# Splitting half of the first part's input weights into fp32r pairs, with the low parts made by GpSimd

## The chip, the cores and the metric

One core of a Trainium2 chip runs the whole program. The metric is the device time of one execution in microseconds; the kernel before was timed three times, with a median of 418.88 us (417.71 to 420.25).

## The reference

```python
# attention: for each of B=4 batches, H=8 heads, S=768 steps, D=48
y[:, :, t] = r_t @ (state + (u * k_t) v_t^T)
state      = w_t[:, None] * state + k_t v_t^T
# then, on x = y as (B*S=3072 rows, 384):
h   = max(x @ w1, x @ w2, x @ w3)        # 384 -> 768
out = h @ w_out                          # 768 -> 384
```

All inputs are float32, except that the four matrices may arrive as float64; the profile is of that form (384 KB a load of 128x384 values).

## The kernel before, in words

The rows of x are worked on in six parts of 512 rows. A part (`half` in the code) needs four chunks of 128 steps of attention. Attention of a chunk k is a list of lettered steps: b, s, f two scans on VectorE, r products of keys and receptances with the scans, d, D, e the diagonal term (e ends with two `affine_select` on GpSimd into `a`), X scores on TensorE, M `copy_predicated` of the scores into `a` on VectorE, T transposes of the keys on TensorE with a ScalarE copy into `kn`, R and V, Z the three products into `y`, U the state's product into `pu`, S its decay on VectorE, E the ScalarE copy of y into x with six small DMAs, n the load of a later chunk's `tin`. V and Z are two passes over the same banks; the first product of Z waits for a `nop` that waits for the last product of V.

The matrix product of a part is cut into 18 groups (a tile f of 128 of the 768 columns, times w1, w2, w3) and the output products behind them. A group's PSUM tile `psm` comes from a pool of three banks. ScalarE copies the first of three groups (L130), VectorE takes the maximum with the other two (L133); this is put out one group later (`behind`). The first part multiplies in plain fp32 (`wval`, `x`, `plain`), three products a group. The other five split x and the weights into a high and a low fp32r part, nine products a group: hi·hi, hi·lo, lo·hi. `split` makes the high part by a ScalarE cast (L110) and the low by a VectorE subtraction (L111).

Each of 24 weight tiles (18 of input, 6 of output) is loaded as raw float64 by SP (`load_w`, letter w), prepared on ScalarE (`split_w1`, L303, letter i), decoded by two VectorE instructions (`split_w2`, L312 and L314; letter c does both for the next one), and later split (`split_w3`, letter f or `fix`). Before, `fix` is called five times behind the groups of the first part, and for the rest in the second part; the loop in `group` spreads the 24 over its 18 groups.

The order on every engine is written out by hand: FRONT for the first chunks, with warm-up products W, then START (letters m for a group, c for a decode, a for a unit of attention), then a loop that puts out groups and units in step. TURN and ORD are a turn of attention cut into units by "|". The `w_p` pool holds raw, decoded and split tiles in a ring.

Of the kernel before, what the change touches and what calls it, by code (L numbers as in the profile page):

```python
# [29 lines left out]
F32 = mybir.dt.float32  # L30
# [4 lines left out]
ALU = mybir.AluOpType  # L35
# [16 lines left out]
HT = 512  # L52
HC = C // 2
CPH = HT // C
SOON = HT - C
# [8 lines left out]
NST = 3  # L64
WARM = 10
XD, LEAD = -2, 0

FRONT = ("b0 s0 f0 d0 W2 D0 W3 r0 X0 T0 W3 c0 e0 b1 s1 d1 D1 U0 f1 W4 R0 e1 M0 V0 Z0 E0 S0 n3 w r1 "  # L70
# [3 lines left out]
TURN = "b1 d1 w | f1 w | D1 r1 c1 | e1 M0 w | "  # L74
ORD = "w R0 V0 U0 X1 Z0 E0 b2 d2 | f2 n3 w | D2 S0 r2 c2 | e2 M1 w | T1 w | |"

# [18 lines left out]
def kernel(ctx: ExitStack, tc, tin, nat, u_flat, u_pair, v_t, w_all, out, ytr):  # L95
# [5 lines left out]

    w_p = ctx.enter_context(tc.tile_pool(name="w", bufs=NW + 1))
    whi, wlo, wval, verdict = [], [], [], []
    acc = const.tile([128, LINE], F32, name="acc")[:, 0:NK]
    wacc = const.tile([128, LINE], F32, name="wacc")[:, 0:NW]
    flag = const.tile([1, LINE], I32, name="flag")[:, 0:1]

    def split(hi, lo, src, later=None):

        nc.scalar.copy(out=hi, in_=src)  # L110
        rest = lambda: nc.vector.tensor_tensor(out=lo, in0=src, in1=hi.bitcast(F32), op=ALU.subtract)  # L111
        rest() if later is None else later.append(rest)
# [4 lines left out]

    def moe_groups(x_hi, x_lo, pools, store, first=0):

# [30 lines left out]
        for f in range(FT):  # L150
            for wi in range(3):
# [10 lines left out]
                ps = ps_m.tile([128, HT], F32, name="psm")  # L162
                n = 0
                for ct in range(KT):
                    terms = ((wval, x_hi),) if plain else ((whi, x_hi), (whi, x_lo), (wlo, x_hi))
                    for wt, xt in terms:
                        nc.tensor.matmul(ps[:, :], lhsT=wt[f * 3 + wi][:, ct * 128:(ct + 1) * 128], rhs=xt[:, ct, :],  # L167
                                         start=(n == 0), stop=(n == KT * len(terms) - 1))
                        n += 1
# [26 lines left out]
    with ExitStack() as fast:  # L196
# [138 lines left out]
        def split_w3(i):  # L335

            w = w_p.tile([128, 2, PC], F32R, name="w")
            whi.append(w[:, 0, :])
            wlo.append(w[:, 1, :])
            split(whi[i], wlo[i], wval[i], wrest)  # L340

# [124 lines left out]
        def transposes(k):  # L466
            if goes_on(k):
                p = prep[k]
                pt = ps_tu.tile([128, 512], F32, name="tu")
                for pr in range(NP):  # L470
# [47 lines left out]
        def values(k, second=False):  # L518
# [16 lines left out]
            if not second and k >= CPH:  # L535
                p["first"] = after(nc.gpsimd.nop(nofuse=True), mm)  # L536

# [51 lines left out]
        def x_parts(half):  # L589
            x = xt[half]  # L590
            if half < PLAIN:
                return x, None
            x_hi = xs_p.tile([128, KT, HT], F32R, name="x_hi")
            x_lo = xs_p.tile([128, KT, HT], F32R, name="x_lo")
            later = []
            for ct in range(KT):
                split(x_hi[:, ct, :], x_lo[:, ct, :], x[:, ct, :], later)
            flush(later)
            return x_hi, x_lo

# [27 lines left out]
        def fix():  # L628
# [3 lines left out]
            if fixed < NW:  # L632
                split_w3(fixed)
            if flush_one:
# [40 lines left out]
        def group():  # L675
            nonlocal groups, mg
            half = groups // GPH
            if groups % GPH == 0 and (half or not mg):
# [9 lines left out]

                mg = moe_groups(*xs[half], pools, store, 0 if half else SOON)
                if half == 0:  # L690
                    return
            g = groups % GPH
            while done < (NW if half or g >= 3 * FT else g + 1):
                weights()
            while half >= PLAIN and fixed <= NW and (half > PLAIN or fixed < 1 + min(NW, -(-(g + 1) * NW // (3 * FT)))):
                fix()
# [192 lines left out]
```

## Time and profile before

| | |
|---|---|
| median of 3 runs | 418.88 us |
| profiled execution, its time | 418.33 us |
| its span, first to last instruction | 416.5 us |
| mean granted TensorE clock | 0.991 |
| TensorE busy | 404.1 us, 97% |
| VectorE busy | 276.7 us, 66% |
| ScalarE busy | 151.1 us, 36% |
| GpSimd busy | 76.2 us, 18% |

The shares are means over the span. In the page, PE is TensorE's products, PEld its weight loads, DVE is VectorE, ACT ScalarE, POOL GpSimd, and a q behind a name is its queue. The first part's groups run from 36.8 to 95.7 us, its output products to 115.2 us.

### The profile page before, as it was taken

How to read it: one execution, taken by the hardware profiler on the slowest of the kernel's cores; microseconds unless marked ns; L12 is line 12 of the kernel's file. 1: busy time of each engine (PE TensorE's matmuls, PEld its weight loads, DVE VectorE, ACT ScalarE, POOL GpSimd, SP SyncE). 2: the span in 40 equal slices, each digit the busy share in tenths (PEclk: the TensorE clock that was granted, in tenths of full speed). 3: DMA queues.
4: the chain of work that ended last, by engine and by line, in shares of the span. 5: the costliest groups of instructions: out<-in, count | busy, mean ns of one | idle time of the engine just before them, and what ended most of it. 6: DMA issues, size and time to landing. Idle time of an engine off the chain costs nothing.

```text
span 416.5 us, 9217 instructions
## 1 busy us (share of the span) xinstructions
PE 404.1 (97%) x3761; PEld 317.9 (76%) x3761; DVE 276.7 (66%) x515; ACT 151.1 (36%) x318; POOL 76.2 (18%) x92
## 2 busy tenths in 40 slices
PE   6989999999999999999999999999999999999995
PEld 3657545546678888987888988889988888888894
DVE  6977998878869968836868558677757532223310
ACT  1343524142545434425334535533623321312211
POOL 3410111013331231311321311421222200000000
PEclk9978999999999999999999999999999999999999
DMA  8982973452380412295644596752460000300002
GB/s 211 329 226 90 331 208 134 133 174 58 88 253 3 126 48 79 61 295 178 201 152 146 121 285 204 210 172 76 134 210 2 2 2 0 97 0 2 1 1 79
DMA packets 23839, 53.30 MB, mean 128 GB/s; under 512 B 3281, under 2 KB 9745, under 8 KB 23793
## 3 DMA queue, kind: packets, MB, share of 16 engines
q1 hardware_dynamic: 19872, 42.65, 33.9%
q10 hardware_dynamic: 3920, 10.03, 7.6%
q8 instruction: 30, 0.49, 0.5%
q14 instruction: 17, 0.13, 0.1%
HBM read 46.77 MB, written 4.72 MB: 124 GB/s over the span
## 4 chain that ended last, share of the span: by engine, by line
PE 90%; DMA 3%; ACT 2%; issue 1%; DVE 1%; SPq 1%; ACTq 0%; DVEq 0%; POOLq 0%
PE psm L167 55%; PE psm L187 14%; PE gram L451 5%; PE y L529 5%; PE tu L494 3%; PE y L484 3%; PE tu L471 2%; PE psm L575 1%; PE psm L413 1%; DMA x<-x 1%; SPq L556 1%; PE psm L147 1%; DMA out_dram<-m 1%; DMA tin<-in_tin_dram 1%; ACT x_hi L110 0%
## 5 line engine op out<-in xcount | busy, mean ns | idle before, releaser
L167 PE MATMUL psm<-x_hi,w 128*128 128x512 f32 x540 | 172.6, 394 | 0.5 <-ACT m L130 0.3
L167 PEld LDWEIGHTS psm<-x_hi,w 128*128 128x128 f32 x540 | 101.4, 188 | 22.6 <-ACT m L191 0.8
L167 PE MATMUL psm<-x_lo,w 128*128 128x512 f32 x270 | 105.2, 390 | 0.0
L133 DVE TENSOR_TENSOR m<-psm,m 128x512 f32<-128x512 f32 x60 | 41.2, 686 | 59.6 <-PE psm L167 44.6
L187 PE MATMUL psm<-w,h_hi 128*128 128x384 f32 x288 | 78.1, 364 | 0.0
L429 POOL TENSOR_SCALAR_AFFINE_SELECT a<-cs 64x512 f32<-64x512 f32 x48 | 37.2, 776 | 159.9 <-DVE cs L423 81.0
L167 PEld LDWEIGHTS psm<-x_lo,w 128*128 128x128 f32 x270 | 50.7, 188 | 9.8
L187 PEld LDWEIGHTS psm<-w,h_hi 128*128 128x128 f32 x288 | 51.8, 188 | 6.5 <-DVE w L314 0.4
L547 ACT COPY x<-y 112x512 f32<-112x512 f32 x24 | 14.1, 586 | 82.0 <-PE y L529 81.6
L167 PE MATMUL psm<-x,w 128*128 128x512 f32 x96 | 43.1, 599 | 0.0
L187 PE MATMUL psm<-w,h_lo 128*128 128x384 f32 x120 | 40.3, 335 | 0.0
L393 ACT ACTIVATE gf<-gf 112x1034 f32<-112x1034 f32 x24 | 25.7, 1070 | 34.4 <-DVE tin L388 34.0
L110 ACT CAST h_hi<-m 128x512 fp32r<-128x512 f32 x30 | 18.6, 622 | 53.7 <-DVE m L133 53.7
L404 POOL TENSOR_TENSOR kr<-kr 128x384 f32<-128x384 f32 x16 | 18.8, 1178 | 92.3 <-PE y L529 87.2
L376 DVE TENSOR_TENSOR_SCAN gf<-tin,d_fwd 112x517 f32<-112x517 f32 x24 | 34.9, 1453 | 0.7
L362 DVE TENSOR_TENSOR_SCAN gf<-tin,d_bwd 112x517 f32<-112x517 f32 x24 | 29.9, 1246 | 5.1 <-DMA tin<-in_tin_dram 5.1
L167 PEld LDWEIGHTS psm<-x,w 128*128 128x128 f32 x96 | 17.6, 190 | 19.5 <-issue 18.9
L111 DVE TENSOR_TENSOR h_lo<-m,h_hi 128x512 fp32r<-128x512 f32 x30 | 20.7, 689 | 17.4 <-ACT h_hi L110 17.4
L460 DVE COPY_PREDICATED a<-mask,gram 128x384 f32<-128x384 int32 x48 | 25.3, 582 | 2.5 <-PE gram L451 2.5
L529 PE MATMUL y<-a,v 64*64 64x128 f32 (+3 forms) x768 | 26.2, 251 | 0.5 <-POOLq L536 0.2
L529 PEld LDWEIGHTS y<-a,v 64*64 64x64 f32 (+1 forms) x768 | 22.2, 129 | 4.8 <-issue 2.4
L130 ACT COPY m<-psm 128x512 f32<-128x512 f32 x30 | 17.5, 582 | 16.6 <-PE psm L167 12.2
(72 smaller groups left out, 424.9 us busy)
## 6 DMA issues: line engine op xcount, KB each, us to landing
tin<-in_tin_dram SPq DMA_DIRECT2D x23, 448.0 KB, 5.6
w<-in_w_all_dram SPq DMA_DIRECT2D x24, 384.0 KB, 7.7
cv<-in_w_all_dram ACTq DMA_DIRECT2D x24, 384.0 KB, 3.4
kr<-in_nat_dram SPq DMA_DIRECT2D x16, 384.0 KB, 5.5
tin<-in_tin_dram SPq DMA_DIRECT2D x23, 231.0 KB, 4.2
v<-in_nat_dram SPq DMA_DIRECT2D x24, 192.0 KB, 6.0
out_dram<-m SPq DMA_DIRECT2D x24, 192.0 KB, 2.1
x<-x SPq DMA_DIRECT2D x30, 32.0 KB, 2.0
```

Of the source, the lines that this page charges most:

```text
L111: rest = lambda: nc.vector.tensor_tensor(out=lo, in0=src, in1=hi.bitcast(F32), op=ALU.subtract)
L133: nc.vector.tensor_tensor(out=m[:, :], in0=ps[:, :], in1=m[:, :], op=ALU.max)
L167: nc.tensor.matmul(ps[:, :], lhsT=wt[f * 3 + wi][:, ct * 128:(ct + 1) * 128], rhs=xt[:, ct, :], start=(n == 0), stop=(n == KT * len(terms) ...
L187: nc.tensor.matmul(pss[tt][:, 0:DM], lhsT=ht[f][:, tok], rhs=wt[FT * 3 + f][:, :], start=(f == 0 and i == 0), stop=(f == FT - 1 and i == l ...
L362: nc.vector.tensor_tensor_scan(out=gf[0:112, 0, ::-1], data0=t[0:112, 0:WC][:, ::-1], data1=d_bwd[0:112, ::-1], initial=0.0, op0=ALU.mult, ...
L376: nc.vector.tensor_tensor_scan(out=gf[0:112, 1, :], data0=tbuf[k % NB][0:112, 0:WC], data1=d_fwd[0:112, :], initial=0.0, op0=ALU.mult, op1 ...
L393: nc.scalar.activation(out=flat, in_=flat, func=AF.Square, accum_out=acc[0:112, k:k + 1])
L404: nc.gpsimd.tensor_tensor(out=n[:, 0, :], in0=n[:, 0, :], in1=n[:, 1, :], op=ALU.mult)
L429: nc.gpsimd.affine_select(out=a[rows, :, 0:2, :], pattern=[[0, 4], [0, 2], [1, HC]], in_=cs[rows, :].rearrange("p (a b) -> p a b", b=2).un ...
L451: nc.tensor.matmul(to, lhsT=p["kp"][q:q + 48, pr, lo:lo + HC], rhs=p["rp"][q:q + 48, pr, HC * late:C], start=(hh, lo) not in begun, stop=T ...
L460: nc.vector.copy_predicated(out=p["a"][:, 2 * hh:2 * hh + 2, :, :].rearrange("p a b c -> p a (b c)"), mask=mask_b(2), data=p["gs"][hh].rea ...
L529: mm = nc.tensor.matmul(p["y"][64 * half:64 * half + m, hh, j, HC * late:C], lhsT=natt[k][0][lo:lo + HC, h * D:h * D + m], rhs=a[:, j, :] ...
```

## The change

In the first part, groups from f = 3 on (weights 9 to 17) multiply split operands, as the later parts do: nine fp32r products in place of three fp32 ones. Their maxima, the intermediate h and the output products of the first part stay plain. The high parts of these nine weights and of the first part's x are cast on ScalarE, the low ones subtracted on GpSimd. x is split ahead of group 6, weight 9 + j ahead of group 7 + j, and for that the decode of weight 10 + j must have been put out. The remaining weights are split later in the order 0 to 8, 18 to 23, by VectorE as before.

Besides: two weight loads in FRONT are put out later; U of a turn moves from its first unit to its third, T from the fifth to the third, behind U; T's bank comes from the pool of the groups for k > 4; the `nop` between V and Z is on SP for chunks 4 to 7; `w_p` has one buffer more.

```diff
+LATE = 3
-FRONT = (... "b0 s0 ... E0 S0 n3 w r1 "
-         "W2 X1 ... S1 w n4 w i i i r2 " ...
-         "W3 X3 d4 T3 R3 M3 x V3 Z3 E3 U3 p p w w ..."
+FRONT = (... "b0 s0 ... E0 S0 n3 r1 "
+         "W2 X1 ... S1 n4 w i i i r2 " ...
+         "W3 X3 d4 T3 R3 M3 x w V3 Z3 E3 w U3 p p w w ..."
-ORD = "w R0 V0 U0 X1 Z0 E0 b2 d2 | f2 n3 w | D2 S0 r2 c2 | e2 M1 w | T1 w | |"
+ORD = "w R0 V0 X1 Z0 E0 b2 d2 | f2 n3 w | D2 U0 T1 S0 r2 c2 | e2 M1 w | w | |"
...
+    late = FT if w_all.dtype == F32 else LATE
+    nl = 3 * (FT - late)
-    def split(hi, lo, src, later=None):
+    def split(hi, lo, src, later=None, eng=nc.vector):
         nc.scalar.copy(out=hi, in_=src)
-        rest = lambda: nc.vector.tensor_tensor(out=lo, in0=src, in1=hi.bitcast(F32), op=ALU.subtract)
+        rest = lambda: eng.tensor_tensor(out=lo, in0=src, in1=hi.bitcast(F32), op=ALU.subtract)
...
+                if plain and f == late:
+                    x_hi, x_lo = parts()
-                    terms = ((wval, x_hi),) if plain else ((whi, x_hi), (whi, x_lo), (wlo, x_hi))
+                    terms = ((wval, x_hi),) if x_lo is None else ((whi, x_hi), (whi, x_lo), (wlo, x_hi))
...
-            split(whi[i], wlo[i], wval[i], wrest)
+            split(whi[i], wlo[i], wval[i], *(None, nc.gpsimd) if 3 * late <= i < 3 * FT else (wrest,))
...
-                pt = ps_tu.tile([128, 512], F32, name="tu")
+                pt = ps_m.tile([128, HT], F32, name="psm") if k > CPH else ps_tu.tile([128, 512], F32, name="tu")
...
-                p["first"] = after(nc.gpsimd.nop(nofuse=True), mm)
+                p["first"] = after((nc.sync if k < 2 * CPH else nc.gpsimd).nop(nofuse=True), mm)
...
+        def split_x(half):
+            x = xt[half]
...
-                split(x_hi[:, ct, :], x_lo[:, ct, :], x[:, ct, :], later)
+                split(x_hi[:, ct, :], x_lo[:, ct, :], x[:, ct, :], later, nc.vector if half else nc.gpsimd)
             flush(later)
...
-                split_w3(fixed)
+                split_w3(fixed + 3 * late if fixed < nl else fixed - nl if fixed < 3 * FT else fixed)
...
-            while half >= PLAIN and fixed <= NW and (half > PLAIN or fixed < 1 + min(NW, -(-(g + 1) * NW // (3 * FT)))):
+            due = nl + g + 1 if nl else -(-(g + 1) * NW // (3 * FT))
+            while half >= PLAIN and fixed <= NW and (half > PLAIN or fixed < 1 + min(NW, due)):
+                fix()
+            if nl and not half and g == 3 * late - 3:
+                split_x(0)
+            while not half and fixed < min(nl, g - 3 * late + 3):
+                while done < min(NW, NW - 13 + fixed):
+                    weights()
                 fix()
```

## Rows read from the trace of the kernel before

**Rows 1.** The page, busy time of each engine over the span.
```profile
PE 404.1 (97%) x3761; PEld 317.9 (76%) x3761; DVE 276.7 (66%) x515; ACT 151.1 (36%) x318; POOL 76.2 (18%) x92
```

**Rows 2.** The chain of waits: start us, length us, what; a stall, plain groups, split groups.
```profile
25.38 1.79 issue
...
66.83 10.50 PE psm L167 x24
...
120.49 10.47 PE psm L167 x45
```

**Rows 3.** Stretches: length, PE, PEld, DVE, ACT, POOL busy, granted clock, DMA share, GB/s.
```profile
57.54:104.40 46.86, 46.86 (x385) 25.06 (x387) 39.87 (x78) 15.64 (x32) 8.57 (x10) 1.00 0.38 119
...
27.16:33.66 6.50, 6.38 (x74) 4.30 (x75) 2.60 (x7) 0.58 (x1) 0.00 (x0) 0.50 0.48 145
...
120.00:180.00 60.00, 60.00 (x551) 51.91 (x542) 48.66 (x87) 26.65 (x57) 13.49 (x16) 1.00 0.31 90
```

**Rows 4.** VectorE's instructions in order of time: start us, length us.
```profile
94.83 1.25 DVE L314 SCALAR_TENSOR_TENSOR w<-w,cv 128x384 uint32<-128x384 uint32 x1
...
98.73 0.56 DVE L314 SCALAR_TENSOR_TENSOR w<-w,cv 128x384 uint32<-128x384 uint32 x1
...
100.22 1.23 DVE L376 TENSOR_TENSOR_SCAN gf<-tin,d_fwd 112x517 f32<-112x517 f32 x1
...
103.35 1.05 DVE L460 COPY_PREDICATED a<-mask,gram 128x384 f32<-128x384 int32 x2
...
183.35 0.69 DVE L133 TENSOR_TENSOR m<-psm,m 128x512 f32<-128x512 f32 x1 [4.06 <-ACT m L130]
...
306.18 1.99 DVE L376 TENSOR_TENSOR_SCAN gf<-tin,d_fwd 112x517 f32<-112x517 f32 x1
```

**Rows 5.** GpSimd's instructions in order of time, beside two of these.
```profile
183.10 1.01 POOL L405 TENSOR_TENSOR kr<-kr,u_bc 128x384 f32<-128x384 f32 x1
...
306.07 1.00 POOL L404 TENSOR_TENSOR kr<-kr 128x384 f32<-128x384 f32 x1 [9.66 <-PE y L529]
```

**Rows 6.** TensorE in order of time, the first product of V.
```profile
104.52 0.57 PE L529 MATMUL y<-a,v 64*64 64x128 f32 x16
```

**Rows 7.** Groups by line and shape: busy us, mean ns, idle before them and releaser.
```profile
L133 DVE TENSOR_TENSOR h_hi<-psm,h_hi 128x512 f32<-128x512 f32 x12 | 8.2, 687 | 4.8 <-PE psm L167 4.7
L460 DVE COPY_PREDICATED a<-mask,gram 128x384 f32<-128x384 int32 x48 | 25.3, 582 | 2.5 <-PE gram L451 2.5
L111 DVE TENSOR_TENSOR w<-w 128x384 fp32r<-128x384 f32 x24 | 13.1, 557 | 3.8 <-ACT w L110 3.8
L110 ACT CAST w<-w 128x384 fp32r<-128x384 f32 x24 | 11.6, 513 | 0.0
L110 ACT CAST x_hi<-x 128x512 fp32r<-128x512 f32 x15 | 8.3, 616 | 1.1 <-DMA x<-x 1.1
```

**Rows 8.** Waits: who for whom, us in total, times, longest us.
```profile
DVE cv L312 <- ACT cv L303: 1.9, 3, 1.0
...
PEld psm L167 <- ACT m L191: 0.8, 1, 0.8
...
PE y L529 <- POOLq L536: 0.2, 1, 0.2
```

**Rows 9.** SP's own waits, the loads of `tin` behind R.
```profile
SPq L241 <- PE y L484: 79.9, 9, 15.1
```

**Rows 10.** SP's issues in order of time, the two loads that move.
```profile
12.41 0.35 SPq L287 DMA_DIRECT2D w<-in_w_all_dram  x1
...
16.02 0.42 SPq L287 DMA_DIRECT2D w<-in_w_all_dram  x1
```

**Rows 11.** The instruction queue in 16.0:16.5, 24.5:25.0 and 30.5:31.0: packets, MB, share of 16 engines.
```profile
q8 instruction: 1, 0.02, 16.0%
q8 instruction: 1, 0.02, 14.3%
q8 instruction: 1, 0.02, 13.0%
```

More of the change, by code (lines that the diff above doesn't have):

```diff
@@ L65 @@
 WARM = 10
+LATE = 3
 XD, LEAD = -2, 0
-FRONT = ("b0 s0 f0 d0 W2 D0 W3 r0 X0 T0 W3 c0 e0 b1 s1 d1 D1 U0 f1 W4 R0 e1 M0 V0 Z0 E0 S0 n3 w r1 "
[1 row of a table removed]
+FRONT = ("b0 s0 f0 d0 W2 D0 W3 r0 X0 T0 W3 c0 e0 b1 s1 d1 D1 U0 f1 W4 R0 e1 M0 V0 Z0 E0 S0 n3 r1 "
[1 row of a table added]
          "W4 X2 d3 D3 T2 c2 b3 s3 e3 R2 U2 n5 w M2 V2 Z2 E2 f3 S2 r3 "
[1 row of a table removed]
[1 row of a table added]
 TURN = "b1 d1 w | f1 w | D1 r1 c1 | e1 M0 w | "
-ORD = "w R0 V0 U0 X1 Z0 E0 b2 d2 | f2 n3 w | D2 S0 r2 c2 | e2 M1 w | T1 w | |"
+ORD = "w R0 V0 X1 Z0 E0 b2 d2 | f2 n3 w | D2 U0 T1 S0 r2 c2 | e2 M1 w | w | |"
 START = ("mcamcamcamcamcamcaamca"
@@ L100 @@
     const = ctx.enter_context(tc.tile_pool(name="const", bufs=1))
-    w_p = ctx.enter_context(tc.tile_pool(name="w", bufs=NW + 1))
-    whi, wlo, wval, verdict = [], [], [], []
+    w_p = ctx.enter_context(tc.tile_pool(name="w", bufs=NW + 2))
+    whi, wlo, wval, verdict = [None] * NW, [None] * NW, [], []
+    late = FT if w_all.dtype == F32 else LATE
+    nl = 3 * (FT - late)
     acc = const.tile([128, LINE], F32, name="acc")[:, 0:NK]
@@ L116, in flush, with moe_groups @@
             later.pop(0)()
-    def moe_groups(x_hi, x_lo, pools, store, first=0):
+    def moe_groups(x_hi, x_lo, pools, store, first=0, parts=None):
         plain = x_lo is None
@@ L337, in split_w3 @@
             w = w_p.tile([128, 2, PC], F32R, name="w")
-            whi.append(w[:, 0, :])
-            wlo.append(w[:, 1, :])
-            split(whi[i], wlo[i], wval[i], wrest)
+            whi[i], wlo[i] = w[:, 0, :], w[:, 1, :]
+            split(whi[i], wlo[i], wval[i], *(None, nc.gpsimd) if 3 * late <= i < 3 * FT else (wrest,))
         wrest = []
@@ L592, in x_parts @@
                 return x, None
+            return split_x(half)
+        xsplit = {}
+        def split_x(half):
+            x = xt[half]
             x_hi = xs_p.tile([128, KT, HT], F32R, name="x_hi")
@@ L596, in x_parts @@
             for ct in range(KT):
-                split(x_hi[:, ct, :], x_lo[:, ct, :], x[:, ct, :], later)
+                split(x_hi[:, ct, :], x_lo[:, ct, :], x[:, ct, :], later, nc.vector if half else nc.gpsimd)
             flush(later)
-            return x_hi, x_lo
+            xsplit[half] = x_hi, x_lo
+            return xsplit[half]
         def run(gen, n):
@@ L687, in store @@
                         tc.mark_branch_hint_location("general", "LikelyTaken", engines=mybir.ALL_ENGINES)
-                mg = moe_groups(*xs[half], pools, store, 0 if half else SOON)
+                mg = moe_groups(*xs[half], pools, store, *() if half else (SOON, lambda: xsplit[0]))
                 if half == 0:
```

4 rows, old and new, of the table FRONT are left out of this document.

## The prediction

> **What bounds the kernel now.** I read the page first: TensorE is busy for 404 of 416.5 us and VectorE, at 66%, is next [rows 1]. The chain of waits then consists almost wholly of TensorE products; in the first 100 us one piece stands out that is none, a stall of 1.79 us at 25.38, named "issue": TensorE stood still and nothing that the profile shows held it [rows 2]. The view by stretches says what the shares hide [rows 3]. In the second part and behind (120 to 180 us) TensorE is busy for all of 60 us, so work that VectorE or ScalarE loses there buys nothing. In the last two thirds of the first part (57.54 to 104.40) TensorE is full too, 46.86 of 46.86 us, but VectorE is at 39.87: it has 6.99 us to spare, and no more. How near it is can be read at the end of that stretch. The last `copy_predicated` there (L460) ends at 104.40 [rows 4] and the first product of V, which needs it, starts at 104.52 [rows 6]. So here both engines are at the limit, and a stretch shortened on TensorE must be shortened on VectorE too.
>
> **The products.** Nine groups change. Four plain groups take 10.50 us, 2.63 each; five split groups take 10.47, 2.09 each [rows 2]. Nine times the difference is 4.8 us off TensorE, all in the stretch named, which it would then fill for 42.1 us. Both prices are from stretches at full granted clock.
>
> **The casts and subtractions.** ScalarE gains nine casts of 513 ns and three of 616 [rows 7], 6.5 us, in a stretch where it is busy for 15.6 of 46.9 [rows 3]. That is hidden. The casts of weight 9 + j come two groups before their use, some 4 us, against a cast of 0.5 and a subtraction of 1.0; without that lead each would cost TensorE those 1.5 us.
>
> GpSimd gains nine subtractions of 128x384 and three of 128x512. The same form on 384 columns takes 1.00 us alone [rows 5], so 9.0 us, and by columns 1.33 each for the others (an estimate), 4.0: 13.0 in all, on an engine busy for 8.6 of the stretch. The cost falls elsewhere. Where a two-input VectorE instruction on SBUF meets such a GpSimd one, it is longer: the scan L376 takes 1.23 alone and 1.99 beside a GpSimd product that began 0.11 earlier, L314 takes 0.56 alone and 1.25 so [rows 4, 5]. I count 18 VectorE instructions that met one; they are 11.1 us longer together than the same forms alone, a mean of 0.62 (the first and the last are the rows). A maximum that reads PSUM (L133) at 183.35, wholly beside one, kept its 0.69 [rows 4, 5].
>
> So VectorE is charged for a part of these 13.0 us. Instructions that read PSUM are taken to be free of it: eight L133 of 687 ns and eight L460 of 582 [rows 7] fall into the stretch, 10.2 of 39.87 us or 26%. The other 74% pay 0.62, so 0.46 per subtraction, and 0.61 per larger one: 9 x 0.46 + 3 x 0.61 = 6.0 us. The bounds: over all 32 GpSimd products of the trace, those that met nothing included, the mean is 0.35, which gives 4.5; if each holds VectorE for its whole length it is 13.0. I take 6.0, near the rows of actual meetings, since VectorE will have few gaps left. Of its idle time 1.9 us are three waits for ScalarE (L303) [rows 8], all in this stretch; I keep 1.0 of them. VectorE then needs 39.87 + 6.0 + 1.0 = 46.9 us, against 42.1 of TensorE. **The stretch takes as long as before, change 0.0**: what TensorE saves it waits for, first for a `psm` bank behind a late maximum, at last for L460 before V. The bounds make this -4.8 (VectorE has no part in it) to +7.9 (39.87 + 13.0 + 1.9).
>
> In the second part VectorE loses nine subtractions of 557 ns [rows 7], 5.0 us, where TensorE has no gap: 0.
>
> **Weight loads later.** Two loads of 384 KB leave the queue at 12.41 and 16.02 [rows 10]; they come back behind the load of chunk 4 and later. No decode waits for a load in this trace, so being later costs nothing. What it might give is the stall at 25.38: an instruction block travels at 24.5, the only one near it. But that block held 14.3% of sixteen engines for half a microsecond, 1.14 us of one, where others had 16.0% and 13.0% [rows 11], in crowded and in quiet queues. Its own transfer isn't what the crowd lengthens by 1.8 us; only its start could be. I take -0.1. If the stall went, so would its consequence: behind it the granted clock is 0.50 (1.2 GHz) for 6.50 us [rows 3]. At 2.4 GHz these would take 3.25 at the least, so 1.79 to 5.0 are in it; I price it at 4.0, and the term's bounds are -4.0 and +0.5.
>
> The Trainium skill ("Runtime: NRT & Kernel Launch", Instruction fetch mechanics) says that fetching instructions is hidden behind the rate of issue in straight code. By that rule the later loads would be worth exactly nothing and the stall something else; the trace, with an "issue" stall of 1.79 us and a block under way in it, speaks against the rule here.
>
> **Order, bank and nop.** T now takes one of three `psm` banks, for 15 chunks, so the group after next finds its bank only if the maximum or copy of the group before T is done: one group of 2.1 us of slack in place of two. TensorE waited 0.8 us once for such a bank (L191) [rows 8]. Nothing below 0 can come of it while TensorE is full; above, 0.8 at each of five part boundaries is 4.0. I take 0.3. U later: its bank and v are held longer, and S waits for U if VectorE is ahead, which is behind TensorE's pace; 0, and 0.5 if that cover is missing. The `nop` on SP: behind it on SP stand the load of `tin` for chunk k + 3, and weights and v. The load of `tin` waits for R of the same unit anyway [rows 9], and V follows R at once, so nobody is later. On GpSimd it would have stood behind the subtractions. It cost 0.2 on TensorE before [rows 8]; 0, bounds -0.2 and +0.5. The `affine_select` pairs now queue behind subtractions on GpSimd, but `a` is needed a whole turn of attention later, which covers the at most three subtractions, 4.0 us, ahead of them.
>
> **Sum**: 418.33 (the profiled execution: span 416.5 and 1.8 around it) + 0.0 - 0.1 + 0.3 = 418.5 us. That execution is 0.55 below the median, inside the spread of the three runs, so I don't correct for it.
>
> **Rivals.**
> *The instruction stall goes.* The lighter queue lets the block start in time, the clock isn't lowered, all behind moves up by 4.0 us: 414.5. For it: VectorE's own gaps there come from the same stall, so it moves up too. Against it: the block's own transfer was no slower than others.
> *TensorE's saving is real.* GpSimd's work falls beside maxima and `copy_predicated`, VectorE pays under 2.2 us: 418.5 - 4.8 = 413.7. For it: a number of products in the trace met nothing. Against it: these met a VectorE with gaps.
> *VectorE becomes the bound: slower.* Where it has no gaps, a subtraction starts just as a VectorE instruction ends and holds the next for its whole 1.00 or 1.33 us. It decides from a charge of 6.0 upward (with 1.0 of waits, the 6.99 are gone); by 0.81 of each length, 10.5, the last L460 comes 4.5 us late, by all 13.0 it comes 7.0 late: 423.0 to 425.5, and nothing later gives it back, since TensorE is full from there. For it: the scan's 0.76 out of a remaining 0.89. Against it: the mean of 0.62. The Trainium skill ("SBUF — State Buffer", SBUF: two separate sides) has this as a rule: the two engines share a pair of ports by an exclusive lock, held for a whole instruction, and the later one fully blocks. The trace agrees in kind; by the rule with no gaps the time would be the upper one.
>
> **How the numbers follow.** Forecast 0.39 (416.8 to 420.9), stall gone 0.23, saving real 0.13, VectorE the bound 0.25. Half a per cent, 2.1 us, is about what a measurement can tell from no change: faster 0.36, same 0.39, slower 0.25. The range reaches from 413.4, into the two faster cases, to 423.2, short of the full lock.
>
> **What would show it.** Right: no TensorE gap between 57 and 105 before, several after, released by VectorE (L133, L460); the split groups of the first part at 2.09 us where they run undisturbed; VectorE near full there, its two-input instructions at 1.2 to 2 times their length beside GpSimd; the stall near 25 us still there. Wrong: VectorE with idle time in that stretch and TensorE without (second rival); no half clock near 30 us (first); the last L460 before the part's end more than 2 us later than 104.4, on the same start (third); new waits on L471's bank or on SP's `nop`.

## The result, and the profile after: 1.3% slower

The changed kernel takes 422.18 us (median of 5 runs, 421.4 to 427.42) against 418.22 us of the kernel before on the same chip (5 runs): ratio 1.013, 95% interval [1.009, 1.018]. The forecast was 418.5 us, and no change the likeliest case; it was slower by some 4 us. The execution that was profiled first is its longest, 427.42 us; a second profile of the same kernel (**after_again** below, 422.22 us) is used for the sums, and the lines shown are of the first unless it says otherwise. Times are medians of all executions of a kernel, while ratios and their intervals leave out the few executions that ran more than 1.5% above that kernel's fastest. Lines of code move down by three to five: L167 is now L172, L133 L136, L111 L114, L312 and L314 are L317 and L319, L507 is L511.

The page of the changed kernel, to be read against [rows 1], with one group of its costliest ones:

```profile
PE 404.3 (95%) x3788; PEld 321.6 (76%) x3788; DVE 277.1 (65%) x506; ACT 152.9 (36%) x321; POOL 98.8 (23%) x104
...
L511 DVE TENSOR_TENSOR scur<-tu,sstar 112x192 f32<-112x192 f32 x13 | 4.6, 355 | 26.0 <-PE tu L498 26.0
```

TensorE's busy time does not fall in this execution, and by 2.3 us in after_again (401.8), although nine groups became cheaper; its share falls: it now has gaps. The second line becomes important further down: VectorE waits 26.0 us for U.

Where the time went is read by stages. In microseconds, from the start of the first part's groups:

| stage | before | after_again | change |
|---|---|---|---|
| start of the first part's groups | 36.67 | 33.83 | -2.84 |
| first part, groups | 59.00 | 61.68 | +2.68 |
| first part, outputs | 19.77 | 19.88 | +0.11 |
| second part, groups | 46.46 | 48.94 | +2.48 |
| third part, groups | 46.44 | 47.47 | +1.03 |
| fourth part, groups | 44.72 | 45.73 | +1.01 |
| fifth part, groups | 46.30 | 46.74 | +0.44 |

The front gives 2.8 us in this pair of profiles (the kernel before has its slow front in some executions only, see **loads_only**), and everything behind it costs more than that. These rows sum to +4.9; the outputs behind the second to the fifth part and the tail make up the rest to the spans' difference of 4.0 (420.5 - 416.5).

The first part's groups by stretches: length, then busy time of PE, PEld, DVE, ACT, POOL, granted clock, DMA share, GB/s. First the kernel before, the whole stage and two pieces of it:

```profile
36.67:95.67 59.00, 58.99 (x483) 31.34 (x481) 52.30 (x99) 22.09 (x43) 8.02 (x9) 1.00 0.60 193
40.00:70.00 30.00, 29.99 (x245) 16.08 (x244) 29.14 (x58) 12.63 (x25) 4.36 (x6) 1.00 0.78 255
70.00:95.67 25.67, 25.67 (x229) 13.26 (x227) 20.02 (x36) 7.97 (x16) 3.67 (x4) 1.00 0.45 139
```

The same view of the changed kernel:

```profile
34.87:96.46 61.59, 57.01 (x494) 37.52 (x492) 56.33 (x96) 27.68 (x56) 23.25 (x22) 0.94 0.51 169
...
71.50:77.50 6.00, 5.99 (x14) 4.74 (x15) 4.95 (x10) 4.82 (x11) 4.86 (x5) 0.51 0.13 53
```

Before, VectorE was busy for 29.14 of the 30 us from 40 to 70, and for 20.02 of 25.67 behind 70. Its spare time lay almost wholly in the second piece. The changed kernel starts to split in the first: x's three subtractions stand at 56.26. GpSimd in order of time (start, length):

```profile
56.26 4.07 POOL L114 TENSOR_TENSOR x_lo<-x,x_hi 128x512 fp32r<-128x512 f32 x3 [13.33 <-issue]
60.28 1.92 POOL L433 TENSOR_SCALAR_AFFINE_SELECT a<-cs 64x512 f32<-64x512 f32 x2
62.28 1.18 POOL L114 TENSOR_TENSOR w<-w 128x384 fp32r<-128x384 f32 x1
```

VectorE in the kernel before, from one maximum (L133) to the next, at the same work:

```profile
55.81 0.68 DVE L133 TENSOR_TENSOR h_hi<-psm,h_hi 128x512 f32<-128x512 f32 x1
...
58.48 0.54 DVE L312 SCALAR_TENSOR_TENSOR cv<-w,cv 128x384 uint32<-128x384 uint32 x1
59.05 0.90 DVE L314 SCALAR_TENSOR_TENSOR w<-w,cv 128x384 uint32<-128x384 uint32 x1
59.88 1.22 DVE L362 TENSOR_TENSOR_SCAN gf<-tin,d_bwd 112x517 f32<-112x517 f32 x1
...
61.67 0.67 DVE L133 TENSOR_TENSOR h_hi<-psm,h_hi 128x512 f32<-128x512 f32 x1
```

VectorE in the changed kernel beside GpSimd's subtractions, and further down at a place in the second part:

```profile
54.27 0.69 DVE L136 TENSOR_TENSOR h_hi<-psm,h_hi 128x512 f32<-128x512 f32 x1
...
57.74 1.45 DVE L317 SCALAR_TENSOR_TENSOR cv<-w,cv 128x384 uint32<-128x384 uint32 x1 [0.67 <-ACT cv L308]
59.23 1.52 DVE L319 SCALAR_TENSOR_TENSOR w<-w,cv 128x384 uint32<-128x384 uint32 x1
60.66 1.00 DVE L317 SCALAR_TENSOR_TENSOR cv<-w,cv 128x384 uint32<-128x384 uint32 x1
61.70 0.90 DVE L319 SCALAR_TENSOR_TENSOR w<-w,cv 128x384 uint32<-128x384 uint32 x1
62.52 2.02 DVE L366 TENSOR_TENSOR_SCAN gf<-tin,d_bwd 112x517 f32<-112x517 f32 x1
64.47 0.73 DVE L405 TENSOR_TENSOR kr<-tin 112x256 f32<-112x256 f32 x2
65.12 0.68 DVE L136 TENSOR_TENSOR h_hi<-psm,h_hi 128x512 f32<-128x512 f32 x1
...
70.68 0.68 DVE L136 TENSOR_TENSOR h_hi<-psm,h_hi 128x512 f32<-128x512 f32 x1
...
127.77 0.36 DVE L511 TENSOR_TENSOR scur<-tu,sstar 112x192 f32<-112x192 f32 x1 [1.79 <-PE tu L498]
...
129.71 0.55 DVE L114 TENSOR_TENSOR w<-w 128x384 fp32r<-128x384 f32 x1
```

And TensorE at the two places:

```profile
68.15 0.40 PE L172 MATMUL psm<-x_hi,w 128*128 128x512 f32 x1
71.51 0.77 PE L172 MATMUL psm<-x_hi,w 128*128 128x512 f32 x1 [2.96 <-DVE h_hi L136]
72.07 0.63 PE L172 MATMUL psm<-x_lo,w 128*128 128x512 f32 x1
72.50 1.05 PE L172 MATMUL psm<-x_hi,w 128*128 128x512 f32 x2
...
130.32 0.73 PE L172 MATMUL psm<-x_hi,w 128*128 128x512 f32 x2 [1.58 <-DVE w L114]
```

Two maxima (L136) that were 5.86 us apart before, at 55.81 and 61.67, are 10.85 apart now, at 54.27 and 65.12. Between them stand the same instructions as before and one more decode, since the split wants its weight decoded earlier (1.1 us by its usual length), a wait of 0.67 for ScalarE's preparation behind the casts of x, and the lengthening beside GpSimd: L317 takes 1.45 for its usual 0.55, L319 1.52 for 0.56, the scan 2.02 for 1.22. The maximum that follows, at 70.68, is late with it, so TensorE, whose groups are shorter by then, stands still for 2.96 us for the bank that it frees. And then the granted clock drops: 0.51 from 71.5 to 77.5, two products that take 0.63 together at full clock take 1.05.

### The profile page after: what moved, and what is told of

It reads as the page before. It is cut to its first block, busy times and chain, and to the rows that moved or that the text cites. A ratio compares the mean times of both kernels' runs of the same rounds, so it can differ in the third digit from the quotient of the medians.

```text
span 425.7 us, 9293 instructions
## 1 busy us (share of the span) xinstructions
PE 404.3 (95%) x3788; PEld 321.6 (76%) x3788; DVE 277.1 (65%) x506; ACT 152.9 (36%) x321; POOL 98.8 (23%) x104
## 4 chain that ended last, share of the span: by engine, by line
PE 78%; DMA 8%; DVE 6%; ACT 3%; issue 3%; SPq 1%; POOL 0%; ACTq 0%; POOLq 0%; DVEq 0%
PE psm L172 45%; PE psm L192 14%; PE y L533 4%; PE gram L455 3%; PE tu L498 3%; PE y L488 2%; PE psm L579 2%; DMA out_dram<-m 2%; DMA v<-in_nat_dram 2%; DMA cv<-in_w_all_dram 2%; DMA w<-in_w_all_dram 2%; PE psm L475 1%; DVE cv L317 1%; ACT x_hi L113 1%; PE psm L150 1%
## 5 line engine op out<-in xcount | busy, mean ns | idle before, releaser
L172 PE MATMUL psm<-x_hi,w 128*128 128x512 f32 x594 | 195.7, 402 | 8.3 <-ACT kn L477 3.4
L172 PEld LDWEIGHTS psm<-x_hi,w 128*128 128x128 f32 x594 | 113.4, 191 | 34.6 <-ACT kn L477 4.0
L172 PE MATMUL psm<-x_lo,w 128*128 128x512 f32 x297 | 117.7, 396 | 0.4 <-DVE x_lo L114 0.4
L136 DVE TENSOR_TENSOR m<-psm,m 128x512 f32<-128x512 f32 x60 | 41.2, 687 | 54.4 <-PE psm L172 46.9
L172 PEld LDWEIGHTS psm<-x_lo,w 128*128 128x128 f32 x297 | 56.9, 192 | 12.3 <-DVE x_lo L114 1.1
L408 POOL TENSOR_TENSOR kr<-kr 128x384 f32<-128x384 f32 x16 | 23.0, 1437 | 81.1 <-PE y L533 80.9
L380 DVE TENSOR_TENSOR_SCAN gf<-tin,d_fwd 112x517 f32<-112x517 f32 x24 | 33.1, 1379 | 0.7
L114 DVE TENSOR_TENSOR h_lo<-m,h_hi 128x512 fp32r<-128x512 f32 x30 | 22.2, 741 | 15.9 <-ACT h_hi L113 15.9
L533 PE MATMUL y<-a,v 64*48 64x64 f32 (+3 forms) x768 | 25.5, 246 | 0.5
L533 PEld LDWEIGHTS y<-a,v 64*48 64x48 f32 (+1 forms) x768 | 21.5, 126 | 4.3 <-issue 2.7
L133 ACT COPY m<-psm 128x512 f32<-128x512 f32 x30 | 17.5, 583 | 16.7 <-PE psm L172 12.3
L192 PEld LDWEIGHTS psm<-w,h_lo 128*128 128x128 f32 x120 | 22.5, 188 | 0.0
L511 DVE TENSOR_TENSOR scur<-tu,sstar 112x192 f32<-112x192 f32 x13 | 4.6, 355 | 26.0 <-PE tu L498 26.0
```

What stands on the lines that cost most here:

```text
L114: rest = lambda: eng.tensor_tensor(out=lo, in0=src, in1=hi.bitcast(F32), op=ALU.subtract)
L136: nc.vector.tensor_tensor(out=m[:, :], in0=ps[:, :], in1=m[:, :], op=ALU.max)
L192: nc.tensor.matmul(pss[tt][:, 0:DM], lhsT=ht[f][:, tok], rhs=wt[FT * 3 + f][:, :], start=(f == 0 and i == 0), stop=(f == FT - 1 and i == l ...
L380: nc.vector.tensor_tensor_scan(out=gf[0:112, 1, :], data0=tbuf[k % NB][0:112, 0:WC], data1=d_fwd[0:112, :], initial=0.0, op0=ALU.mult, op1 ...
L408: nc.gpsimd.tensor_tensor(out=n[:, 0, :], in0=n[:, 0, :], in1=n[:, 1, :], op=ALU.mult)
L533: mm = nc.tensor.matmul(p["y"][64 * half:64 * half + m, hh, j, HC * late:C], lhsT=natt[k][0][lo:lo + HC, h * D:h * D + m], rhs=a[:, j, :] ...
```

## The experiments

Each kernel was timed in five rounds beside the kernel before. Ratios are to that, as recorded with their intervals; they are not the quotients of the medians given here (early_due's medians alone would give 1.004, for 1.0085), so a difference of half a per cent between two kernels is shown only where their intervals part or a stage shows it. The theory to be tested: VectorE, lengthened where it has no slack, is what TensorE waits for. Its rivals: the second part's splits; the turn with T's bank; the loads; ScalarE's casts.

**only_split.** The change without its loads and its turn:

```diff
-FRONT, ORD as in the changed kernel; pt = ps_m... if k > CPH else ps_tu...
+FRONT, ORD as before; pt = ps_tu.tile([128, 512], F32, name="tu")
```

> The split of weights 9 to 17 alone, with the order of loads, the turn and the bank of the transposes as before. If VectorE's sharing with GpSimd eats the saving (the forecast): 418 to 421 us, TensorE waits of 4 to 5 us between 57 and 105 us released by VectorE's maxima, none by the copy of kn. If the turn and the bank are what costs: the split alone saves, 413 to 416 us, with less than 1 us of waits there.

421.45 us, ratio 1.0075 [1.004, 1.011]. The split alone is slower: against before its profile has +2.2 us in the first part's groups (61.19) and +1.5 in the second's (47.98), and no gain at the front (37.23). Its third part takes 47.38, 0.9 above before, with neither the new turn nor the new bank.

**no_split.** The change without the split:

```diff
-LATE = 3
+LATE = 6
```

> The changed kernel without the split (the first part plain again, all 24 weights split later by VectorE), with the late loads, the new turn, T in the pool of the groups and the nop on SP. If the split is the cost: 415 to 418 us, the front 1.5 us shorter and no new waits behind it. If the turn and the bank are the cost: 420 to 424 us, with waits of TensorE for the copy of kn of 2 to 3 us at the start of the third part and VectorE waiting 15 us or more for U.

418.4 us, ratio 1.0009 [0.9985, 1.0033]. The rest of the change costs, by itself, about what its front gives: the groups start at 33.25, and the first part takes 60.27 where **loads_only**, below, takes 58.96. The fourth and the fifth part have the whole +1.0 and +0.4 of the table (45.70 and 46.73) without any split. The fifth part's belongs to the new turn: it takes 46.73 to 46.76 in every kernel with it and 46.3 in every one without. Of the fourth part's, old_turn below keeps 0.6 (45.35).

**old_turn.** The change with the turn as before, T in its own bank again:

```diff
-ORD = "w R0 V0 X1 Z0 E0 b2 d2 | f2 n3 w | D2 U0 T1 S0 r2 c2 | e2 M1 w | w | |"
+ORD = "w R0 V0 U0 X1 Z0 E0 b2 d2 | f2 n3 w | D2 S0 r2 c2 | e2 M1 w | T1 w | |"
-pt = ps_m.tile([128, HT], F32, name="psm") if k > CPH else ps_tu.tile(...)
+pt = ps_tu.tile([128, 512], F32, name="tu")
```

> The changed kernel with U in the first unit, T in the fifth and T's bank back in its own pool. If the turn and the bank cost what the two profiles show behind the first part: 4 to 7 us less than the changed kernel in the same state, 415 to 418 us, VectorE's waits for U back from 26 to about 2 us. If the split in the first part is all of it: 421 to 423 us as the changed kernel.

419.66 us, ratio 1.0047 [1.0015, 1.0078]: 0.6 to 0.9% better than the changed kernel by their ratios, some 2.5 to 3.6 us. VectorE's wait of 26.0 us for U (L511) is 2.1 again, as before the change, and the third part takes 45.95 (the kernels with the old turn reach from 45.87 to 47.38 there). The first part stays at 61.10:

```profile
34.85:95.95 61.10, 55.53 (x510) 36.17 (x508) 58.84 (x99) 27.71 (x56) 22.95 (x22) 1.00 0.52 170
```

**early_due.** The change with the splits of the second part put out three groups earlier:

```diff
-due = nl + g + 1 if nl else ...
+due = nl + g + 4 if nl else ...
```

> The changed kernel with each weight of the second part split three groups earlier. If TensorE's wait of 1.6 us there comes from splits put out just in time: that wait goes and the time falls by 1 to 2 us. If it comes from VectorE being late as a whole (its wait for U in front): the wait moves or stays, change under 0.5 us.

419.69 us, ratio 1.0085 [1.0047, 1.0123]. The second part takes 46.64, with 48.98 in the changed kernel and 46.46 before, so its +2.5 us are the splits that come out just in time. In the changed kernel's lines above: the subtraction at 129.71 stands behind the wait for U (1.79 us, to 127.77) and the products of step r, and TensorE waits 1.58 us for its weight at 130.32. As whole times, this kernel and the changed one don't part clearly (their intervals overlap); **due_and_turn** and old_turn, which differ by the same line alone, do.

**loads_only.** The kernel before with the two loads moved:

```diff
-... Z0 E0 S0 n3 w r1 ... S1 w n4 w i i i r2 ... M3 x V3 Z3 E3 U3 p p w w
+... Z0 E0 S0 n3 r1 ... S1 n4 w i i i r2 ... M3 x w V3 Z3 E3 w U3 p p w w
```

> The kernel before with the order of FRONT of the changed one, so the weight loads later and nothing else. If the late loads shorten the front (the forecast's first rival): the first group of products starts at 33 to 35 us in place of 36.7 and the time falls by 1.5 to 3.5 us, to 414.5 to 416.5. If the shorter front came from something else: no change, 417.5 to 418.5.

417.18 us, ratio 0.9986 [0.9959, 1.0012]: not told apart from no change. In its profile the "issue" stall is 1.03 us at 25.48 for 1.79, no half clock follows, and the groups start at 33.77. The two pieces in its chain of waits:

```profile
25.48 1.03 issue
...
33.94 2.26 PE psm L147 x7
```

So the stall was shorter by 0.8 us and the start came 2.9 earlier in this execution, while the median fell by 0.6 to 0.9 us. The kernel before has the half clock in only some of its executions: 6.50 us at 0.50 [rows 3] lower an execution's mean clock by 0.008 (an estimate: half of 6.50, of 416.5), and 18 of its 141 executions beside the experiments have a mean of 0.998 or more, so they can't have had it. Their median is 415.2 us; of the 45 with a mean of 0.990 to 0.992 it is 419.0. With the later loads 5 of 12 executions have 0.998 or more, so an undisturbed front is more frequent with them, but the half clock is not gone: **late5**, with the same loads, had it. These five have a median of 417.2, 2 us above the 415.2, so the later loads also seem to cost something; what, no run shows.

**spare_pool.** The kernel before with twelve GpSimd subtractions that nobody uses, at the changed kernel's places in the program. On the chip x's three run earlier, at 45.13 for 56.26, since no cast holds them:

```diff
+if not half and g == 6:
+    for ct in range(KT):
+        spare(xt[0][:, ct, :], HT)
+if not half and 7 <= g <= 15:
+    spare(wval[g - 7], PC)
```

> The kernel before with twelve subtractions on GpSimd whose results nobody uses (three of 512 columns ahead of group 6, nine of 384 ahead of groups 7 to 15), and no split. If sharing with GpSimd alone makes VectorE late: VectorE's instructions in the first part are 5 to 7 us longer together, the three large ones take 3 to 4 of it within 9 us, TensorE waits for a maximum there, and the part's 59.0 us of groups grow by 0.5 to 2.5. If the lateness comes from casts and decodes ahead of the split and not from sharing: under 2 us longer and the part within 0.3 of 59.0.

419.68 us, ratio 1.0048 [1.0018, 1.0079]. With nothing changed on TensorE and VectorE, the subtractions alone cost 1.4 us in the first part's groups:

```profile
37.26:97.63 60.37, 59.24 (x481) 31.25 (x480) 58.50 (x99) 22.08 (x43) 20.03 (x21) 1.00 0.59 188
```

VectorE's busy time rises from 52.30 to 58.50 with the same 99 instructions: 6.2 us for twelve subtractions, 4.8 of them hidden in slack. That is the contention by itself, in the size that the prediction gave it.

**on_vector** and **x_on_vector.** old_turn with all twelve subtractions on VectorE, or x's three alone:

```diff
-split(whi[i], wlo[i], wval[i], *(None, nc.gpsimd) if ...)      # on_vector only
+split(whi[i], wlo[i], wval[i], *(None, nc.vector) if ...)
-split(x_hi[:, ct, :], ..., later, nc.vector if half else nc.gpsimd)
+split(x_hi[:, ct, :], ..., later, nc.vector)                    # both
```

> The changed kernel with the old turn and bank, and all twelve low parts on VectorE itself. These are 9 x 0.46 + 3 x 0.6 = 6 us of VectorE work in place of some 6 us of lengthening. If VectorE's total is what bounds the first part: as with GpSimd, 61 us of groups, within 1 us of it. If the bunching of the three large ones on GpSimd is what costs (4 us within 9): shorter by 1.5 us or more, 59.5 or less.

421.96 us, ratio 1.0139 [1.0092, 1.0186].

> The same, with only x's three low parts on VectorE and the weights' nine on GpSimd. If the three large ones cost 4 us on GpSimd and 1.8 on VectorE: the wait of TensorE for a maximum behind group 9 (3 us) falls to 1 us or less and the groups of the first part take 1 to 2 us less than 61.1. If VectorE's total decides: within 0.7 us of 61.1.

420.42 us, ratio 1.0085 [1.0047, 1.0123]; the first part's groups take 61.73, no shorter than old_turn's 61.10. VectorE's busy time in the first part's groups is nearly the same whichever engine subtracts: 58.84 in old_turn, 58.37 with x's three moved, 58.55 with all twelve. Moving them to GpSimd therefore relieves VectorE of nothing here. on_vector's stage is nevertheless the longest, 64.64 (at a clock of 0.95), since a subtraction on VectorE that waits for its cast holds everything behind it; three lines of its waits:

```profile
PE psm L172 <- DVE h_hi L136: 6.3, 2, 4.8
PEld psm L172 <- ACT w L113: 5.2, 1, 5.2
...
DVE w L114 <- ACT w L113: 2.9, 2, 1.7
```

So this pair bounds the contention only loosely: a second thing, the wait for casts, changed with it.

**after_again.** The changed kernel unchanged:

> The changed kernel once more, for a second trace beside the next three. If its time is the sum of its parts (front -2 to -3, groups of the first part +2, of the second +2, later parts +1 to +3 from the turn and the bank): 420 to 423 us, with these stages in the trace. If the first trace was typical in its 3 us waits at the third part's start: 425 or more.

422.47 us, ratio 1.0108 [1.0074, 1.0143]. The extra 5 us of the first profile are mostly one place: its third part takes 50.98, here 47.47. There T's product sat in a bank until ScalarE copied it (L477), and ScalarE was behind a load (`cv`, 8.39 us) that an earlier instruction in its queue needed. TensorE waits 2.79 us at 196.47, and behind it two products take 1.05 us again, so the clock has dropped. The chain of waits of the first profile there:

```profile
180.62 5.19 DMA out_dram<-m
...
185.93 8.39 DMA cv<-in_w_all_dram
...
194.74 0.74 ACT cv L338 x2
...
195.88 0.54 ACT kn L477
```

**half_decode** and **half_decode_before.** old_turn, and the kernel before, with one decode instruction left out for every second weight:

```diff
-nc.vector.scalar_tensor_tensor(out=low, in0=hi, scalar=0x80000000, in1=low, ...)
+if i % 2 == 0:
+    nc.vector.scalar_tensor_tensor(out=low, in0=hi, scalar=0x80000000, in1=low, ...)
```

> The changed kernel with the old turn and bank, and with the first of the two decode instructions left out for every second weight, so 12 VectorE instructions of 551 ns less, about ten of them in the groups of the first part (the values of these weights are then not the reference's). If VectorE's total bounds that stage: it falls by 4 to 5 us, from 61.1 to 56 or 57, towards TensorE's 54.2. If casts on ScalarE or the subtractions' lateness bound it: less than 1.5 us.

417.79 us, ratio 0.9985 [0.9957, 1.0013].

> The kernel before with the same left out. TensorE bounds its first part: the stage stays at 59.0, within 0.3, and the time within 1 us of the kernel before. If VectorE bounds it already: 1 to 4 us less.

418.02 us, ratio 0.9987 [0.995, 1.0023]. The kernel before has nothing to gain from a lighter VectorE, as [rows 3] say of a full TensorE. With the split, VectorE's busy time falls by 4.9 us (58.84 to 53.92), and the stage by only 1.06. The big wait stays, 2.90 us at 70.43. The reason stands in VectorE's lines of half_decode:

```profile
53.34 0.68 DVE L136 TENSOR_TENSOR h_hi<-psm,h_hi 128x512 f32<-128x512 f32 x1
...
56.81 1.44 DVE L318 SCALAR_TENSOR_TENSOR cv<-w,cv 128x384 uint32<-128x384 uint32 x1 [1.27 <-ACT cv L308]
58.28 2.44 DVE L320 SCALAR_TENSOR_TENSOR w<-w,cv 128x384 uint32<-128x384 uint32 x2
60.65 1.68 DVE L367 TENSOR_TENSOR_SCAN gf<-tin,d_bwd 112x517 f32<-112x517 f32 x1
62.25 2.29 DVE L406 TENSOR_TENSOR kr<-tin 112x256 f32<-112x256 f32 x2
64.46 0.68 DVE L136 TENSOR_TENSOR h_hi<-psm,h_hi 128x512 f32<-128x512 f32 x1
```

The two maxima are 11.12 us apart, 10.85 in the changed kernel, though two decode instructions between them are gone. VectorE comes to ScalarE's preparation earlier and waits 1.27 us for it, for 0.67. And L406, which took 0.73, now takes 2.29, beside two subtractions that GpSimd does from 61.33 to 64.25: while GpSimd works through its subtractions, the VectorE instructions that come next are the long ones, except the maximum, which reads PSUM and keeps its 0.68. My account by VectorE's total fell with this run; what counts is where the subtractions, and the casts ahead of them, stand.

**due_and_turn.** old_turn with early_due's line; the base of the kernels below.

> The changed kernel with the old turn and bank, and each weight of the second part split three groups earlier. If the second part's loss is the splits put out just in time: its groups go from 48.0 back to 46.5 us, and what is left is the front's gain against the first part's loss: 417.5 to 419. If VectorE is late there for another reason: 48 stays, 419 to 420.5.

417.40 us, ratio 0.998 [0.995, 1.0011]. The two repairs add: second part 46.39, third 45.87. The first part's groups still take 60.85.

**lows_on_scalar.** due_and_turn with the twelve low parts written by a second ScalarE cast, so that no GpSimd instruction is added (they hold the value itself, and the difference is never formed):

```diff
+if eng is nc.gpsimd:
+    nc.scalar.copy(out=lo, in_=src)
+    return
```

> due_and_turn with the twelve low parts of the first part written by a second ScalarE cast in place of a GpSimd subtraction (they then hold the value itself, so the numbers are not the reference's; TensorE's work is the same). If sharing between GpSimd and VectorE is the cause: VectorE's 6 us of lengthening go, and the groups of the first part take 54.5 to 57 us in place of 60.9, the time 411 to 414. If ScalarE's queue (casts between decodes) is the cause: 60 or more, since ScalarE does more.

411.95 us, ratio 0.9891 [0.985, 0.9931]. The first part's groups:

```profile
34.02:90.18 56.16, 54.52 (x509) 36.22 (x508) 52.34 (x99) 32.98 (x68) 8.19 (x10) 1.00 0.56 190
```

This is the strongest test: 60.85 falls to 56.16, 4.7 us, and VectorE from 58.03 to 52.34, by 5.7, on the same instructions. About 1.0 of the 4.7 is clock: due_and_turn's stage ran at 0.97 and old_turn's, with the same work, at 1.00, with TensorE busy for 56.54 and 55.53. It also shows what the split is worth alone: TensorE is busy for 54.52, 4.47 less than before. A wait of 1.64 at the same group stays (3.32 in due_and_turn), behind a wait of VectorE for ScalarE's preparation (2.24 us, to 58.18). So GpSimd made about half of that wait or more; the rest comes from the casts and the decode brought forward, and here also from the second casts. In all, some 2.8 of the 59.0 are won.

**x_spread**, **late4_spread**, **late4** and **late5** keep the subtractions on GpSimd and move them. x_spread splits x one tile ahead of each of groups 3, 4 and 5; late4 and late5 split only 6 or 3 weights, x ahead of group 9 or 12; late4_spread is x_spread and late4 together. The edits of late5 and the core of x_spread, to due_and_turn:

```diff
-LATE = 3
+LATE = 5
-while done < min(NW, NW - 13 + fixed):
+while done < min(NW, NW - 8 + fixed):
...
-if nl and not half and g == 3 * late - 3:       # x_spread
-    split_x(0)
+if nl and not half and 3 <= g < 3 + KT:
+    split_x(0, g - 3)
```

> due_and_turn with x split one column tile at a time ahead of groups 3, 4 and 5, in place of all three ahead of group 6. If the bunch at groups 6 to 10 is the cause: the wait of 3.3 us for a maximum there falls under 1.5 and the groups of the first part take 57.5 to 59.5 us. If VectorE's total decides: 60 to 61.5, the wait only moves.

418.38 us, ratio 1.0021 [0.9993, 1.0049]: first part's groups 60.77, no better.

> The same with the split from f = 4 on, six weights in place of nine. TensorE's saving is 3.2 us then, VectorE's lengthening some 4.5. If VectorE's total decides: 59 to 60.5 us in the first part's groups. If the bunch was the cause and is gone: 56 to 58, and a time under 416.

417.57 us, ratio 1.0006 [0.9979, 1.0033]: 58.93.

> due_and_turn with the split from f = 4 on, x split ahead of group 9 and six weights ahead of groups 10 to 15. If lengthening is paid only where VectorE has no slack: x's three subtractions now fall behind 65 us, the first part's groups take 56.5 to 58 us (TensorE saves 3.2 of 59.0) and the time is 414 to 416. If every lengthening is paid wherever it falls: 59.5 or more, 417.5.

416.29 us, ratio 0.9967 [0.9933, 1.0]: 57.94.

> The same from f = 5 on, x split ahead of group 12 and three weights ahead of groups 13 to 15. TensorE saves 1.6 of 59.0. If lengthening is covered behind 70 us: 57.5 to 58 us and 415 to 416.5. If it is paid wherever it falls: 60 or more, 418.

415.22 us (413.71 to 416.65), ratio 0.9945 [0.9916, 0.9973]: faster than the kernel before, and than the changed one. Spreading x earlier puts it where VectorE is full, and gains nothing; moving it to where the windows above have VectorE's gaps (from 68.0 us in late4, 72.9 in late5) gains. The cleanest pair is late4 and late4_spread, which split the same six weights and differ in x's place alone: 1.0 us in the stage, though their whole times don't part clearly. late5 also has fewer subtractions, six for twelve. late5's first part, and GpSimd in it:

```profile
37.74:95.08 57.34, 57.34 (x491) 32.99 (x489) 52.56 (x95) 24.90 (x49) 16.37 (x16) 1.00 0.55 181
```

```profile
72.93 4.36 POOL L114 TENSOR_TENSOR x_lo<-x,x_hi 128x512 fp32r<-128x512 f32 x3 [1.40 <-DMA w<-in_w_all_dram]
82.02 2.46 POOL L114 TENSOR_TENSOR w<-w 128x384 fp32r<-128x384 f32 x2 [4.72 <-ACT w L113]
```

TensorE is full, 57.34 of 57.34, and all of the three groups' saving, 1.65 us, arrives, although VectorE is lengthened by 5.9 us in 50 to 106 us against 1.9 before (1.2 of the 5.9 behind the groups, at 105). In its profile the front has the old stall (1.65 us at 25.17) and a clock of 0.56 from 26.0 to 37.7, so its span of 414.9 us is without the front's gain.

**bank_only.** due_and_turn with T's bank from the groups' pool, in the old order:

```diff
-pt = ps_tu.tile([128, 512], F32, name="tu")
+pt = ps_m.tile([128, HT], F32, name="psm") if k > CPH else ps_tu.tile([128, 512], F32, name="tu")
```

> due_and_turn with T's bank in the pool of the groups and the old order of the turn. If the bank is what the new turn costs in the parts behind: waits of TensorE for the copy of kn at the parts' starts and 1.5 to 3 us more than due_and_turn. If the late U is (VectorE waiting for it): within 0.7 us of due_and_turn.

423.12 us, ratio 1.013 [1.0086, 1.0174]: 5.7 us above due_and_turn. The first part takes 62.60 for its groups and 21.88 for its outputs (60.85 and 19.40). TensorE's waits that are new:

```profile
PE psm L475 <- ACT m L196: 2.5, 2, 1.9
...
PE psm L172 <- ACT kn L477: 1.4, 1, 1.4
```

T now takes its turn among three banks: it waits until an output is copied out, and the groups wait until T is. With the later U and earlier T of the change, the bank costs less than this alone; together, by old_turn, 2.5 to 3.6 us. The fourth and the fifth part take 44.79 and 46.29 here, so what the changed kernel loses in these (45.73 and 46.74) hangs on the new order and not on the bank alone. No run has the new order without the bank.

## Why the prediction was wrong, step by step

**The products: right in size.** -4.8 us were forecast; where the twelve subtractions are absent (lows_on_scalar) TensorE's busy time in the first part's groups is 4.47 less, and late5's three groups give 1.65, 0.55 each.

**The charge on VectorE: right in size, 6.0.** Over 50 to 106 us VectorE's instructions are 7.7 us longer than their usual lengths in the changed kernel (13 of them), 1.9 before (5): 5.8. spare_pool has 6.2; old_turn, reckoned in the same way, has 9.4, so 7.5 more than before. Five of the 18 meetings behind the mean of 0.62 are L370, a one-input instruction of 0.17 us that was held for 0.4 to 0.8, so the price is not one of two-input instructions alone.

**"The stretch takes as long as before, change 0.0": this step failed.** It set the charge against 6.99 us of spare time as if they could be spent anywhere between 57.54 and 104.40. The row in [rows 3] had one number for the whole stretch; cut at 70 us it reads:

```profile
57.54:70.00 12.46, 12.46 (x119) 6.56 (x118) 12.25 (x27) 4.57 (x10) 2.95 (x4) 1.00 0.44 144
70.00:104.40 34.40, 34.40 (x268) 18.50 (x270) 27.61 (x52) 11.07 (x23) 5.62 (x7) 1.00 0.36 110
```

VectorE has 0.21 us to spare in the first piece and 6.79 in the second. The subtractions of x, and the first of the weights', stand in the first. TensorE therefore waited 2.98 us at one group (after_again), 4.98 in the whole stage, and the clock fell behind that wait (0.62 from 69 to 78 us), so that TensorE was busy for 56.7 us, where old_turn at full clock has 55.5 and lows_on_scalar 54.5: 54.5 + 1.0 (between these two, not explained) + 1.2 (the clock) + 5.0 = 61.7, for 59.0. late5 and lows_on_scalar show it from both sides. Two parts of the wait I hadn't priced at all: the decode brought forward (1.1 us) and ScalarE's preparation late behind the casts of x (0.67), since I looked at ScalarE's mean of 15.6 in 46.9.

**Rival "VectorE becomes the bound: slower"** named the right engine and sign, and its time (423.0 to 425.5) is above what came. Its point of decision, a charge of 6.0 upward, was worked out from the same pool. Single instructions did behave by its rule, held for a whole 0.9 us, and in sum the charge stayed at the forecast's.

**Second part, 0: failed, +2.5 us.** I counted VectorE's work there, nine subtractions fewer, and not when the remaining splits come out. The new line `due = nl + g + 1` puts each cast out one group ahead of its use and the subtraction only with the group that uses it, so a subtraction behind a wait for U and other work makes TensorE wait. early_due takes it back.

**Bank, order and nop, +0.3: too small.** Undoing turn and bank is worth 2.5 to 3.6 us; the bound of 4.0 held. I argued that U later costs nothing because VectorE is behind TensorE's pace; in the later parts it isn't, and it waits 26.0 us for U. How much of the loss is that wait's is not shown: bank_only loses more with U early (2.1 us of waits). `nop` was not tried by itself; late5, which has it on SP, takes 46.39, 45.87, 44.71 and 46.29 us in the second to the fifth part, none longer than before, so no cost of it shows.

**Weight loads, -0.1: not shown to be wrong.** In the profiles of no_split and the changed kernel the groups start at 33.2 to 34.9, for 36.7, but the whole time gains 0.6 to 0.9 us by loads_only, which is not clear of 0, and the bounds of -4.0 to 0.5 held. The rival that the stall goes was half right: executions without the half clock are more frequent with the later loads, and by late5 it doesn't go reliably. (The stall is not the only piece of the early chain that is no product, as the prediction has it: a load of 3.19 us stands at its start. Nothing rests on that.)

**Sum for after_again**: front -2.8, first part +2.7, second +2.5, turn and bank in the third to the fifth part +2.5, the rest -0.8: +4.0, where I had -0.1, 0, 0 and 0.3. The third part's share of the turn's 2.5, 1.0 us, lies within what the kernels with the old turn differ by there. That the miss is no larger is luck: the front's -2.8 stands against +7.7 behind it, and it is the difference between an execution before with the half clock and one after without.

## What to carry to other kernels

Slack is a place, not a sum: before handing work to an idle engine that slows a busy one, cut the busy engine's idle time into stretches no longer than the buffers can bridge (here two groups, 4 to 5 us at 2.09 to 2.63 each) and put the work where the gaps are. When a change renumbers or reorders, recompute by how much each producer is ahead of its consumer, even in stages whose total load falls. A PSUM bank borrowed by an operation that another engine must empty puts that engine's queue into TensorE's path.

## What the runs showed of the hardware that I had not expected

VectorE pays the same whether it subtracts itself or GpSimd does beside it: 58.55 and 58.84 us of busy time in the same stage. The Trainium skill ("SBUF — State Buffer", section "SBUF: two separate sides") says that the two share ports by an exclusive lock; the trace agrees in kind, with L317 at 1.45 for 0.55 us, and half_decode shows that the price passes to the next instruction in line (2.29 for 0.73) when two are taken out.

A wait of 3 us can cost more than itself. Behind 2.96 us in the changed kernel the granted clock was 0.51 (1.2 GHz) for 6 us, and behind 2.79 at 196.47 the products were slower too; behind 3.32 us in old_turn and 2.90 in half_decode it stayed at 1.00, while behind the same 3.32 at the same group in due_and_turn two products took 1.05 us for 0.62. What decides between them these runs don't show.
